# Copying a chunk's two banks of down sums with two engines instead of one

## The chip, the cores and the metric

The kernel runs on one core of a Trainium2 chip. The core has five engines that run side by side, each with its own queue of instructions in program order: TensorE (PE; its weight loads are listed apart as PEld), VectorE (DVE), ScalarE (ACT), GpSimd (POOL) and SyncE (SP). Here SP and POOL issue transfers. The metric is the device time of one execution in microseconds; the time of a kernel is the median over its runs.

## The reference

Two layers in a row, in float32. First an attention through 49 agents for each of 4 batches of 12480 rows of 128 numbers, then a feed-forward layer over all 49920 rows.

```python
def _attn_ref(q, k, v, agents):
    scale = 1.0 / np.sqrt(q.shape[-1])
    ...
    a2k = sm(agents, k)          # softmax over the keys
    agent_v = a2k @ v            # 49 x 128 per batch
    q2a = sm(q, agents)          # softmax over the agents
    return (q2a @ agent_v).astype(np.float32)

def _moe_ref(x, w_in, w_out):
    h = x @ w_in                                  # 128 -> 2048
    g = h * (1.0 / (1.0 + np.exp(-1.702 * h)))
    return (g @ w_out).astype(np.float32)         # 2048 -> 128
```

## The kernel before

The rows are taken in 98 chunks of 512 (`CH`), two chunks to a group. The last chunk has 256 rows. Within a group 16 steps are counted (`NF`), eight to a chunk, and the program is written two steps at a time by `two_steps(t)`. Each step multiplies a chunk's softmaxed queries up to 128 x 2 of the 2048 inner numbers (`up`, PSUM tiles `ph`), ACT applies the gate (`g`, L557), and four steps later (`LAG = 4`) `down` multiplies them back to 128 outputs. The sums of a chunk's eight down steps gather in the PSUM tile `po`.

Products are kept near float32 by splitting an operand in a rounded part and the rest: `gh` is the rounded `g`, made by a POOL transfer (L564) or by an ACT copy (L566), and `gl = g - gh` is made by DVE (L572), 776 times in all. `down` then does three products: `gh` with `wo_h`, `gl` with `wo_h`, `gh` with `wo_l`.

`po` has two banks. PE works with two halves of its rows at once: rows 0 to 63 of the contraction add into bank 0, rows 64 to 127 into bank 1, so a chunk's result is the sum of both banks. `po` has one buffer, so the first `down` of the next chunk can't write before the banks of this one have been read. `store` reads them: ACT copies both (L599, 128 x 1024) into the SBUF tile `o`, SP writes the first half of `o` to memory (L600), and three steps later POOL adds the second half to it in memory with a transfer that accumulates (`store_add`, L605).

The order on each engine is the order in which this Python code runs (`manual_schedule`). Between the last `down` of a chunk and the first of the next, PE has one pair of `up` calls, and at some boundaries more: after an odd chunk the query transposes (L527), after an even chunk the query scores (L216). Other work is put at given steps by `put`: the splits and scores of the queries (L201, L203, L216, L229), the softmax (L503, L507, L513), and for the next batch first the key scores (steps in `K_AT`) and then the value sums (`v_pair`, `e_pair`, `acc`). So an engine's program differs from chunk to chunk, and the same pattern comes three times, once per batch; in the last fifth there is no next batch.

Chunks are counted from 0 below. In DVE's queue the place of `store` lies behind a `gl` of the chunk that ends and ahead of another `gl`, `gl` being made by

```python
    def second(t, f):
        jobs(t + 1)
        if FIRST + 2 <= t < steps + 2:
            do_low(t - 2)
```

which `two_steps` calls between the last two `down` of the chunk; `store` follows both.

Of the kernel before, what the change touches and what calls it, by code (L numbers as in the profile page):

```python
# [45 lines left out]
def kernel(  # L46
# [10 lines left out]
    nc = tc.nc  # L57
# [14 lines left out]
    def width(m):  # L72
        return min(CH, T - m * CH)
# [516 lines left out]
    def store(m, po):  # L590
        n = width(m)
        o = work.tile([P, 2, CH], F32, name="o", tag="o", bufs=1)[:, :, :n]
        out = outT[:, m * CH : m * CH + n]
        if m == NC - 1:
            nc.scalar.copy(out=o[:, 0], in_=po[:, 0, :n])
            nc.vector.tensor_add(out=o[:, 0], in0=po[:, 1, :n], in1=o[:, 0])
            nc.sync.dma_start(out=out, in_=o[:, 0])
            return None
        nc.scalar.copy(out=o, in_=po[:, :, :n])  # L599
        nc.sync.dma_start(out=out, in_=o[:, 0])  # L600
        return o

# [97 lines left out]
    with tc.manual_schedule(engines={E.PE, E.Activation, E.DVE, E.Pool, E.SP}):  # L700
# [9 lines left out]
        for c in range(2):  # L710
            nc.vector.tensor_add(
                out=sel[:, c * H : c * H + A], in0=ident[:, 0:A], in1=ident[:, H : H + A]
# [150 lines left out]
    po = {}  # L863
# [8 lines left out]
    def two_steps(t):  # L872
# [34 lines left out]
        if not downs:  # L907
            second(t, f)
        elif e == NF // 2 - 2:
            put(t + 3, lambda m=m, o=store(m, po.pop(m)): store_add(m, o))  # L910
# [53 lines left out]
```

## Time and profile before

| | us |
|---|---|
| median of 3 runs | 1939.64 |
| lowest and highest run | 1938.58, 1943.8 |
| profiled execution (its span, first to last instruction) | 1941.2 |
| PE busy | 1895.0 (98%) |
| DVE busy | 1538.4 (79%) |
| ACT busy | 1500.1 (77%) |
| POOL busy | 328.2 (17%) |
| chain that ended last: PE's share | 85% |
| mean granted TensorE clock | 0.996 |

The profile is of one execution; its span lies 1.6 us above the median of the runs, and no other time is given for it. Busy time of PE is modelled from its matmuls, which overlap, so 98% doesn't say that PE did all it could. Where PE did nothing while waiting for another engine, the list of waits has it, with the engine and line that ended the wait.

### The profile page before, as it was taken

The page shows a single profiled execution, that of the slowest core. Times are in us where ns is not written, and L with a number is a line of the kernel's source. Part 1 is how long each engine was busy: PE and PEld are TensorE (multiplying, and loading weights), DVE is VectorE, ACT ScalarE, POOL GpSimd, SP SyncE. Part 2 cuts the span into 40 slices and gives each one's busy share as a digit, 9 for nine tenths or more (in the row PEclk, how much of TensorE's full clock was granted, in tenths as well). Part 3 has the DMA queues.
Part 4 walks back from the last instruction along what each step waited for, and adds up shares of the span by engine and source line. Part 5 has one row for each costly group of instructions (what it writes and reads, how often), then busy time and mean ns, then how long its engine had stood idle before and what let it go on. Part 6 is the DMA issues. An engine that isn't in the chain of part 4 may idle for free.

```text
span 1941.2 us, 56369 instructions
## 1 busy us (share of the span) xinstructions
PE 1895.0 (98%) x24100; PEld 1588.5 (82%) x24100; DVE 1538.4 (79%) x1979; ACT 1500.1 (77%) x2414; POOL 328.2 (17%) x583
## 2 busy tenths in 40 slices
PE   7899999999999999999999999999999999999998
PEld 4577788878799998788789999788878888888887
DVE  6798988878688889888778988888877667666665
ACT  3677777887788777877787778777877788888886
POOL 0011111111111111111111111111111111111112
PEclk9999999999999999999999999999999999999999
DMA  8477776776567776776657677777555666666665
GB/s 337 143 220 218 208 195 191 206 202 204 170 205 205 210 209 185 208 205 198 196 175 210 206 211 203 193 202 200 184 169 180 183 193 186 199 188 193 187 181 144
DMA packets 133213, 383.39 MB, mean 198 GB/s; under 512 B 14998, under 2 KB 17174, under 8 KB 132962
## 3 DMA queue, kind: packets, MB, share of 16 engines
q0 software_dynamic: 77264, 253.00, 45.3%
q1 hardware_dynamic: 55697, 126.78, 21.1%
q8 instruction: 189, 3.10, 0.7%
q14 instruction: 63, 0.51, 0.1%
HBM read 81.53 MB, written 50.99 MB: 68 GB/s over the span
## 4 chain that ended last, share of the span: by engine, by line
PE 85%; DVE 5%; ACT 3%; issue 2%; DMA 1%; POOL 0%; ACTq 0%; DVEq 0%; POOLq 0%
PE po L109 52%; PE ph L109 25%; PE ps_m L216 5%; DVE gl L572 2%; PE ps_m L109 1%; ACT g L557 1%; ACT o L599 1%; DMA gh<-g 1%; PE ps_m L473 1%; DVE v_pair L422 1%; DVE rest L203 0%; PE ps_m L527 0%; DVE rest L201 0%; DVE v_pair L421 0%; DVE lo L538 0%
## 5 line engine op out<-in xcount | busy, mean ns | idle before, releaser
L557 ACT ACTIVATE g<-ph 128x512 f32<-128x512 f32 x1568 | 809.4, 605 | 326.4 <-PE ph L109 319.8
L572 DVE TENSOR_TENSOR gl<-g,gh 128x1024 fp32r<-128x1024 f32 x776 | 920.1, 1213 | 58.0 <-DMA gh<-g 38.0
L109 PE MATMUL po<-gh,wo_h 64*128 64x512 f32 (+1 forms) x3104 | 512.8, 400 | 16.6 <-ACT o L599 15.5
L109 PE MATMUL po<-gl,wo_h 64*128 64x512 f32 (+1 forms) x3104 | 502.6, 394 | 1.5 <-DVE gl L572 1.5
L109 PE MATMUL po<-gh,wo_l 64*128 64x512 f32 (+1 forms) x3104 | 498.0, 391 | 0.0
L564 POOL DMA_DIRECT2D gh<-g x436 | 236.5, 542 | 1510.3 <-ACT g L557 1227.5
L566 ACT CAST gh<-g 128x1024 fp32r<-128x1024 f32 (+1 forms) x340 | 359.7, 1058 | 9.2
L109 PEld LDWEIGHTS po<-gl,wo_h 64*128 64x128 f32 x3104 | 311.0, 185 | 58.6 <-DVE gl L572 8.0
L109 PEld LDWEIGHTS po<-gh,wo_l 64*128 64x128 f32 x3104 | 312.8, 185 | 54.2
L109 PEld LDWEIGHTS po<-gh,wo_h 64*128 64x128 f32 x3104 | 296.6, 186 | 68.1 <-ACT o L599 19.1
L109 PE MATMUL ph<-hi,wh 49*128 49x512 f32 (+4 forms) x1616 | 330.3, 388 | 0.0
L109 PE MATMUL ph<-lo,wh 49*128 49x512 f32 (+4 forms) x1616 | 329.6, 388 | 0.0
L109 PE MATMUL ph<-hi,wl 49*128 49x512 f32 (+4 forms) x1616 | 327.5, 384 | 0.0
L109 PEld LDWEIGHTS ph<-hi,wh 49*128 49x128 f32 x1616 | 167.5, 185 | 30.8 <-issue 2.4
L109 PEld LDWEIGHTS ph<-hi,wl 49*128 49x128 f32 x1616 | 166.1, 186 | 26.6 <-issue 0.9
L109 PEld LDWEIGHTS ph<-lo,wh 49*128 49x128 f32 x1616 | 165.7, 184 | 24.9
L599 ACT COPY o<-po 128x1024 f32<-128x1024 f32 x97 | 98.3, 1013 | 53.4 <-PE po L109 53.4
L538 DVE TENSOR_TENSOR lo<-ps_m,hi 128x256 fp32r<-128x256 f32 x98 | 37.0, 420 | 120.7 <-ACT hi L536 120.7
L203 DVE TENSOR_TENSOR rest<-rest 128x512 bf16<-128x512 f32 (+2 forms) x176 | 129.3, 742 | 0.9
L216 PE MATMUL ps_m<-ag_part,rest 64*128 64x49 bf16 x4188 | 118.9, 181 | 5.2 <-DVE rest L203 5.0
L216 PEld LDWEIGHTS <-rest 64*128 64x128 bf16 (+1 forms) x4236 | 109.7, 94 | 6.0 <-DVE rest L203 5.8
L605 POOL DMA_DIRECT2D outT<-o x97 | 84.9, 876 | 93.1 <-DMA outT<-o 80.9
(140 smaller groups left out, 1305.4 us busy)
## 6 DMA issues: line engine op xcount, KB each, us to landing
gh<-g POOLq DMA_DIRECT2D x432, 512.0 KB, 3.5
kt<-kT SPq DMA_DIRECT2D x52, 480.0 KB
outT<-o SPq DMA_DIRECT2D x97, 256.0 KB
outT<-o POOLq DMA_DIRECT2D x97, 256.0 KB, 5.5
qt<-qT SPq DMA_DIRECT2D x94, 256.0 KB
vt<-v SPq DMA_DIRECT2D x39, 480.0 KB
hi<-hi SPq DMA_DIRECT2D x98, 98.0 KB
lo<-lo SPq DMA_DIRECT2D x98, 98.0 KB
```

The lines of the kernel that those rows point to most:

```text
L109: nc.tensor.matmul(out=out, lhsT=lhsT[r], rhs=rhs[r], start=start, stop=stop, tile_position=(k * H, 0))
L203: nc.vector.tensor_sub(out=halves(r)[1][:, s], in0=r[:, s], in1=halves(r)[0][:, s])
L216: nc.tensor.matmul(out=ps[k][o : o + n, j * A : (j + 1) * A], lhsT=x[r, t0 : t0 + n], rhs=ag_part[r, b, y, :], start=(i == 0), stop=(i == ...
L422: nc.vector.tensor_sub(out=vp[:TB, :, C : 2 * C], in0=vt[:TB], in1=vp[:TB, :, 0:C].bitcast(F32))
L473: nc.tensor.matmul(out=pw[:, i * 256 : i * 256 + m], lhsT=w["avT"], rhs=w_in_sb[:, t : t + m], start=True, stop=True)
L538: nc.vector.tensor_sub(out=l, in0=x, in1=h.bitcast(F32))
L557: nc.scalar.activation(out=g[:, k, :n], in_=ph[k][:, :n], func=AF.Gelu_apprx_sigmoid)
L564: nc.gpsimd.dma_start(out=gh, in_=g)
L566: nc.scalar.copy(out=gh, in_=g)
L572: nc.vector.tensor_sub(out=gl, in0=g, in1=gh.bitcast(F32))
L599: nc.scalar.copy(out=o, in_=po[:, :, :n])
L605: nc.gpsimd.dma_start(out=outT[:, m * CH : m * CH + width(m)], in_=o[:, 1], accum_op=ALU.add)
```

## The change

The one copy of both banks by ACT becomes two: ACT copies bank 0, DVE copies bank 1. The transfers out and the last chunk's store are as before. The new line shifts the line numbers behind it by one: the SP store is L601 in the changed kernel, POOL's L606.

```diff
-        nc.scalar.copy(out=o, in_=po[:, :, :n])
+        nc.scalar.copy(out=o[:, 0], in_=po[:, 0, :n])
+        nc.vector.tensor_copy(out=o[:, 1], in_=po[:, 1, :n])
         nc.sync.dma_start(out=out, in_=o[:, 0])
         return o
```

DVE's queue at the end of an odd chunk in the last fifth of the program, before (`p_pad` is the softmax result, `gl` the rest of `g`, `lo` the rest of the transposed queries; names in brackets are the engines and transfer queues whose semaphores an instruction waits for):

```order
L513 TENSOR_TENSOR p_pad<-e_sb,z 128x2x4x49 [waits DVE_49]
L572 TENSOR_TENSOR gl<-g,gh 128x1024 [waits DMASW6_49,PE_49]
L572 TENSOR_TENSOR gl<-g,gh 128x1024 [waits DMASW7_49,PE_49]
L538 TENSOR_TENSOR lo<-ps_m,hi 128x4x64 [waits DMAHW0_49,DMAHW1_49,PE_49,Activation_49]
L538 TENSOR_TENSOR lo<-ps_m,hi 128x4x64
```

And at the same kind of place now:

```order
L513 TENSOR_TENSOR p_pad<-e_sb,z 128x2x4x49 [waits DVE_49]
L572 TENSOR_TENSOR gl<-g,gh 128x1024 [waits DMASW1_49,PE_49]
L600 COPY o<-po 128x512 [waits DMAHW2_49,DMASW7_49,Activation_49]
L572 TENSOR_TENSOR gl<-g,gh 128x1024 [waits DMASW2_49]
L538 TENSOR_TENSOR lo<-ps_m,hi 128x4x64 [waits DMAHW0_49,DMAHW1_49,PE_49,Activation_49]
L538 TENSOR_TENSOR lo<-ps_m,hi 128x4x64
```

The copy stands between two `gl`. It waits for the transfers that read `o` the last time and for ACT; PE isn't among its waits. The count of ACT's semaphore that it waits for is the one that SP's store of bank 0 (L601) waits for, that of ACT's copy.

PE's queue where the next chunk's sums begin, before (`po` is the new chunk's tile; the two rows ahead are the query transposes):

```order
L527 MATMUL ps_m<-ident,p_pad 128x64 [waits DVE_49,PE_49]
L527 MATMUL ps_m<-ident,p_pad 128x64 x7
L109 MATMUL po<-gh,wo_h 128x512 [waits DMASW3_49,Activation_49]
L109 MATMUL po<-gh,wo_h 128x512 x3
L109 MATMUL po<-gl,wo_h 128x512 [waits DVE_49]
L109 MATMUL po<-gl,wo_h 128x512 x3
L109 MATMUL po<-gh,wo_l 128x512 x4
```

And now:

```order
L527 MATMUL ps_m<-ident,p_pad 128x64 [waits DVE_49,PE_49]
L527 MATMUL ps_m<-ident,p_pad 128x64 x7
L109 MATMUL po<-gh,wo_h 128x512 [waits DMASW3_49,DVE_49]
L109 MATMUL po<-gh,wo_h 128x512 x3
L109 MATMUL po<-gl,wo_h 128x512 x4
L109 MATMUL po<-gh,wo_l 128x512 x4
```

The first product of a chunk waited for ACT and waits for DVE now; the products with `gl` have no wait of their own here any more, since DVE's copy stands behind that `gl`. Beside these rows the queues of PE, ACT, DVE, POOL and SP hold the same instructions in the same order, with ACT's copy half as wide.

## Rows read from the trace of the kernel before

**Rows 1.** The page's busy times: us, share of the span, instructions.

```profile
PE 1895.0 (98%) x24100; PEld 1588.5 (82%) x24100; DVE 1538.4 (79%) x1979; ACT 1500.1 (77%) x2414; POOL 328.2 (17%) x583
```

**Rows 2.** PE's waits: who waited for whom, us in total, times, longest us.

```profile
PE po L109 <- ACT o L599: 15.5, 20, 1.7
...
PE po L109 <- DVE gl L572: 1.5, 5, 0.3
```

**Rows 3.** Groups of ACT by line and shape: count, busy us, mean ns, idle before.

```profile
L599 ACT COPY o<-po 128x1024 f32<-128x1024 f32 x97 | 98.3, 1013 | 53.4 <-PE po L109 53.4
...
L292 ACT COPY e_col<-ps_m 120x512 f32<-120x512 f32 x12 | 7.1, 588 | 15.5 <-PE ps_m L290 15.4
```

**Rows 4.** Groups of DVE, the same columns.

```profile
L434 DVE COPY acc<-ps_m 128x514 f32<-128x514 f32 x3 | 2.1, 687 | 0.0
...
L375 DVE COPY run_max<-score 120x392 f32<-120x392 f32 x3 | 1.1, 359 | 0.0
```

**Rows 5.** Timeline, ACT handing to DVE: start, duration, instruction, [idle before <-releaser].

```profile
920.99 0.48 ACT L228 COPY e_sb<-ps_m 128x392 f32<-128x392 f32 x1
...
921.50 0.57 DVE L229 TENSOR_TENSOR e_sb<-ps_m,e_sb 128x392 f32<-128x392 f32 x1 [2.18 <-ACT e_sb L228]
```

**Rows 6.** Timeline at the end of chunk 43, which is odd.

```profile
934.32 2.35 DVE L572 TENSOR_TENSOR gl<-g,gh 128x1024 fp32r<-128x1024 f32 x2
...
936.45 1.01 ACT L599 COPY o<-po 128x1024 f32<-128x1024 f32 x1
...
937.51 0.73 PE L109 MATMUL po<-gh,wo_h 64*128 64x512 f32 x4 [0.74 <-ACT o L599]
```

**Rows 7.** Timeline at the end of chunk 73, odd, in the last fifth.

```profile
1522.01 1.22 DVE L572 TENSOR_TENSOR gl<-g,gh 128x1024 fp32r<-128x1024 f32 x1
...
1523.89 1.01 ACT L599 COPY o<-po 128x1024 f32<-128x1024 f32 x1
...
1524.95 0.73 PE L109 MATMUL po<-gh,wo_h 64*128 64x512 f32 x4
```

**Rows 8.** The same boundary, DVE alone: what follows the two `gl`.

```profile
1527.43 0.76 DVE L538 TENSOR_TENSOR lo<-ps_m,hi 128x256 fp32r<-128x256 f32 x2 [4.21 <-ACT hi L536]
```

**Rows 9.** The last such boundary, chunk 93.

```profile
1878.23 1.00 ACT L599 COPY o<-po 128x1024 f32<-128x1024 f32 x1
...
1879.28 0.49 PE L109 MATMUL po<-gh,wo_h 64*128 64x512 f32 x2
```

**Rows 10.** Timeline at the end of chunk 0.

```profile
88.81 2.35 DVE L572 TENSOR_TENSOR gl<-g,gh 128x1024 fp32r<-128x1024 f32 x2
...
89.01 0.73 PE L109 MATMUL po<-gh,wo_h 64*128 64x512 f32 x4 [1.66 <-ACT o L599]
```

**Rows 11.** Timeline at the end of chunk 3.

```profile
147.96 1.02 ACT L599 COPY o<-po 128x1024 f32<-128x1024 f32 x1 [0.27 <-PE po L109]
...
148.79 2.35 DVE L572 TENSOR_TENSOR gl<-g,gh 128x1024 fp32r<-128x1024 f32 x2
...
149.37 0.48 PE L109 MATMUL po<-gh,wo_h 64*128 64x512 f32 x1
```

**Rows 12.** Timeline at the end of chunk 25.

```profile
584.27 2.35 DVE L572 TENSOR_TENSOR gl<-g,gh 128x1024 fp32r<-128x1024 f32 x2
584.42 1.02 ACT L599 COPY o<-po 128x1024 f32<-128x1024 f32 x1 [0.32 <-PE po L109]
...
585.78 0.48 PE L109 MATMUL po<-gh,wo_h 64*128 64x512 f32 x1
```

**Rows 13.** Timeline at the end of chunk 34, where value sums begin.

```profile
763.14 2.35 DVE L572 TENSOR_TENSOR gl<-g,gh 128x1024 fp32r<-128x1024 f32 x2
...
763.81 0.93 PE L109 MATMUL po<-gh,wo_h 64*128 64x512 f32 x4
```

**Rows 14.** Windows: us, busy us (instructions) per engine, granted clock, DMA share, GB/s.

```profile
760.00:764.00 4.00, 2.47 (x106) 1.92 (x104) 3.96 (x7) 3.54 (x6) 0.53 (x1) 1.00 0.93 294
764.00:768.00 4.00, 4.00 (x22) 3.13 (x22) 3.93 (x6) 0.49 (x1) 0.88 (x1) 0.57 0.83 198
```

## The prediction

> **What bounds the kernel now.** I read the busy times first, then PE's waits, then the timeline at the chunk ends. PE is busy for 1895.0 of 1941.2 us and DVE and ACT for 79% and 77% [rows 1], so PE sets the time and a microsecond counts only where PE has to wait longer or less long. In PE's waits the line that the change touches comes first: 15.5 us over 20 occasions in which the first product of a new chunk waits for ACT's copy L599; DVE's `gl` costs PE next to nothing, 1.5 us [rows 2]. Those 15.5 us are all that a faster emptying of `po` can give back. One of the 20 is the wait of 1.66 us at the start [rows 10], one of 0.4 us lies near the end, and the 18 others are one pattern, 0.74 us each [rows 6]: six odd chunks in each of the three stretches in which the next batch's value sums are made. There ACT comes late, since its copy starts without an idle time before it. 18 times 0.74 is 13.3 us, which with the two others makes the 15.4.
>
> **What the change does to one boundary.** ACT's copy goes from 128 x 1024 to 128 x 512. The old one takes 1.013 us on average; a 512-wide ACT copy out of PSUM is in the trace and takes 0.588 [rows 3]. So the ACT half ends 0.43 us sooner. DVE gets a copy of 512 out of PSUM. The nearest row is a DVE copy of 514 out of PSUM, 0.687 us; the fastest DVE copy rate in the trace is that from SBUF, 392 elements in 0.359, which for 512 would be at most 0.47 [rows 4]. I take 0.69, the row with the same source and size, and keep 0.47 as the low end. The Trainium skill (VectorE: DVE Perf Modes, "Why PSUM operands drop a tier") says that a float32 operand in PSUM holds VectorE to its base rate; the two rows agree with that, and by it alone the low end would fall away.
>
> The two copies look as if they ran side by side. In the new program they don't: DVE's copy waits for ACT's semaphore at ACT's copy, and PE's first product now waits for DVE. The new chain from the start of ACT's copy is therefore 0.59 (ACT), some 0.03 for the handing over (ACT's copy L228 ends at 921.47, DVE's add starts at 921.50 [rows 5]), and 0.69 (DVE): 1.31 us where it was 1.02. The release comes **0.29 us later**, if DVE is free. If DVE is still at work on the `gl` ahead of the copy, it comes later still: 0.69 us after that `gl`, whatever ACT does. PE starts about 0.05 after the release (the old copy ends at 937.46, PE starts at 937.51 [rows 6]).
>
> **The sum over the 97 boundaries**, each by the same rule:
> - The 18 odd chunks with ACT late. The `gl` ahead of the copy is the first of the two at 934.32, done by 935.54, so DVE is waiting when ACT's half ends at 937.04, and its copy ends at 937.76 [rows 6]. PE waits 0.29 more: 18 x 0.29 = 5.2 us.
> - Twelve odd chunks of the last fifth, from 71 to 93. PE starts the new chunk at 1524.95, just 0.05 behind the end of the old copy at 1524.90 [rows 7], and so in the last of them, 1879.28 behind 1879.23 [rows 9]. Nothing is to spare: 12 x 0.29 = 3.5 us.
> - Three odd chunks of the opening, 3, 5 and 7, with DVE late. The first of two `gl` that begin at 148.79 ends near 150.01 (half of the pair); DVE's next instruction starts 0.08 before the end of the last, so the copy runs from 149.93 to 150.62, and PE could start at 150.67 where it started at 149.37: 1.30 each, 3.9 us [rows 11]. Chunk 0 the same way: `gl` until 90.03, PE at 90.69 for 89.01, 1.68 [rows 10]. Chunks 1 and 2 come to 2.0 together.
> - Eight odd chunks like 25 (25 to 31, 49 to 55), where the key scores fill DVE: `gl` until 585.49, PE at 586.15 for 585.78, 0.37 each, 2.9 us [rows 12].
> - Chunks 10, 34, 58 and 40. In 34 the first `gl` ends at 764.36, so PE starts at 765.02 for 763.81, 1.21 [rows 13]; the four together are 3.8 us.
> - The last three and one more: 0.7 us.
> - The other 45 or so, nearly all even: PE has the query scores or the key scores to do between two chunks and reaches the new one later than the new release. They cost nothing.
>
> Together 5.2 + 3.5 + 3.9 + 1.7 + 2.0 + 2.9 + 3.8 + 0.7 = **23.7 us**. With the copy at 0.47 us the same sum is 13.
>
> **What lies beside other work.** ACT gives back 97 x 0.43 = 41 us of busy time, which is worth nothing: it doesn't bring the late copies forward, because between two of them ACT sits idle for PE, 53.4 us ahead of L599 alone [rows 3]. DVE takes on 97 x 0.69 = 67 us, 82% of the span, and also stands still until ACT is done. Behind the waiting copy in its queue is a `gl`, then `lo`, scores or splits. At chunk 73 that `gl` now starts at 1522.01 next to its neighbour and would start near 1525.1, three microseconds later; but the instruction behind it, `lo`, waits for ACT until 1527.43 anyway [rows 7, 8], so the delay ends there. At every boundary I followed the added delay until DVE's next idle time and found no `gl` and no split that PE would have to wait for beyond what the late release already costs. That cover is thinnest at the odd chunks. Queues: the SP store of bank 0 leaves 0.43 us sooner; POOL's accumulating transfer waits for that store's landing and so is not held up by DVE's copy.
>
> The sum stands against the profiled execution of 1941.2 us, and since that lies 1.6 above the median of the runs I add it to the median: 1939.6 + 24 = 1964.
>
> **Rivals.**
> - *The copies overlap after all* (the wait for ACT would be for something older). The Trainium skill (PSUM — Partial Sum Buffer, "Specifications (TRN2)") says that ScalarE and VectorE read PSUM in parallel at full rate if their banks differ, as they do here. No row before shows the two at it; the order of waits speaks against it, not the memory. In numbers of this kernel: at the 18 late chunks the release comes 0.43 sooner, 18 x -0.43 = -7.7; the twelve would not lose their 3.5; the 14.3 us of the chunks where DVE is late stay, since DVE's place in its queue is the same. Net +6.5: 1946.
> - *DVE's lateness spreads, or PE's clock falls.* Where PE had little to do around 762, waiting twice and working on narrow score products, its granted clock went to 1.2 GHz for a while: 0.57 on average from 764 to 768, full before [rows 14]. Such a fall costs (1 - 0.57) x 4 = 1.7 us. The waits of 0.74 didn't bring one, nor did that of 1.66. After the change there are about 25 waits between 1.0 and 3.4 us. If half or all of them brought a fall, that is 20 to 43 us on top; DVE falling behind in the opening, where its slack is smallest, would add some 10. About 1990.
> - *Faster.* The side that could win is the 18 late chunks: ACT's half frees bank 0 at 937.04 instead of 937.46. If the wait for DVE turned out short there (a copy side by side) and the later releases made room in which DVE is no longer behind at the others, -7.7 to at most -15.5 us would be left: 1924 to 1932. It decides as soon as the chunks with DVE late lose less than 7.7 us in all; I count 14.3 for them, and each rests on a `gl` that ends after ACT's half would.
> - *Nothing to measure.* PE's times are modelled and small waits may be absorbed in them; with the overlap above and half of DVE's lateness gone, the sum is near 0: 1940.
>
> **How the numbers follow.** A change of under 0.3%, some 6 us, can't be told from none here. The forecast, 1964, has a chance of 0.62, with 1953 (the quick copy) to 1976 as its own range. DVE or the clock getting worse: 0.17. The overlap: 0.10, half of it within 6 us and half above. Faster: 0.05. Nothing: 0.06. So slower 0.62 + 0.17 + 0.05 = 0.84, the same 0.11, faster 0.05. The range from 1946 to 1988 takes in the overlap and part of the clock case.
>
> **What would show it.** In the changed kernel's profile the DVE copy should take 0.69 us and start right behind the end of ACT's copy at odd chunks; PE's waits for DVE's copy should come to some 40 us (15.5 + 24) in about 50 places, those for ACT's copy should be gone, and the waits for `gl` stay small. If the DVE copies start together with ACT's, the chain is wrong. If PE's waits for `gl` or for the splits grow by more than 5 us, the cover that I counted is not there. If the clock row shows more stretches at half speed than before, the second rival is at work.

## The result and the profile after

| | before | after |
|---|---|---|
| median of 4 runs each, us | 1939.11 | 1967.34 |
| lowest and highest | 1937.99, 1943.8 | 1963.1, 1969.33 |
| ratio, with 95% interval | | 1.0135 [1.0121, 1.0149] |
| profiled execution's span, us | 1941.2 | 1964.9 |

The changed kernel is slower by 28 us at the median. The two profiled spans are only 23.7 us apart, because the profiled execution of before was one of its longer ones. A run's span, from the first to the last instruction, is 1.8 us shorter than its time (1964.9 for the 1966.71 of the profiled run of after), so the 1941.2 us stand for a time of some 1943 us; the difference has to do with PE's clock and is taken up below.

The busy times of after answer to [rows 1]:

```profile
PE 1899.9 (97%) x24100; PEld 1547.2 (79%) x24100; DVE 1601.2 (81%) x2076; ACT 1462.4 (74%) x2414; POOL 326.7 (17%) x583
```

DVE has 97 more instructions and 63 us more of work, ACT 38 us less, and PE's work is the same to 5 us. PE's waits answer to [rows 2] (who waited for whom: us in total, times, longest us):

```profile
PE po L109 <- DVE o L600: 34.2, 41, 3.3
PE ps_m L216 <- DVE rest L203: 3.7, 5, 1.0
...
PE po L109 <- DVE gl L572: 1.1, 4, 0.3
```

The 15.5 us of waiting for ACT's copy are gone from the list, and 34.2 us of waiting for DVE's copy stand in their place, in 41 places instead of 20. Waits for `gl` haven't grown.

The next two fences are ACT's and DVE's copies in the groups by line and shape (columns as in [rows 3]):

```profile
L599 ACT COPY o<-po 128x512 f32<-128x512 f32 x97 | 56.6, 584 | 52.6 <-PE po L109 52.6
```

```profile
L600 DVE COPY o<-po 128x512 f32<-128x512 f32 x97 | 66.7, 688 | 79.9 <-ACT o L599 79.9
```

The last figures of the two lines matter most: how long the engine stood idle ahead of the copies, and what ended it. ACT's copy waits for PE, as before. DVE's copy is put down to ACT alone, 79.9 us over the kernel. So the two copies run one behind the other, and in a timeline this looks as follows. Chunk 43, the boundary of [rows 6]:

```profile
950.02 1.22 DVE L572 TENSOR_TENSOR gl<-g,gh 128x1024 fp32r<-128x1024 f32 x1
...
952.15 0.58 ACT L599 COPY o<-po 128x512 f32<-128x512 f32 x1
...
952.76 0.69 DVE L600 COPY o<-po 128x512 f32<-128x512 f32 x1 [1.52 <-ACT o L599]
...
953.50 0.73 PE L109 MATMUL po<-gh,wo_h 64*128 64x512 f32 x4 [1.03 <-DVE o L600]
```

From the start of ACT's copy to PE's first product it is 953.50 - 952.15 = 1.35 us; in [rows 6] it was 937.51 - 936.45 = 1.06. That is the 0.29 us of the prediction, and PE's wait went from 0.74 to 1.03. DVE had been idle for 1.52 us, waiting for ACT.

To see where the time went, I took the start of the last `down` product of each chunk in either trace and subtracted. The shift grows at few places:

| boundary (chunk that ends) | forecast, us | shift added, us |
|---|---|---|
| ahead of the first chunk boundary | 0 | 1.9 |
| 0, the wait | 1.68 | 1.66 |
| 0, PE at a lower clock behind the wait | 0 | 1.5 |
| 1 and 2 | 2.0 | 1.4 |
| 3, 5, 7 | 3.9 | 3 x 0.65 = 1.95 |
| 18 odd chunks with ACT late, 12 of the last fifth | 8.7 | 8.6 |
| 8 like chunk 25 | 2.9 | 8 x 0.36 = 2.9 |
| 10, 34, 58, 40 | 3.8 | 3.0 |
| 56 and the rest | 0.7 | 1.1 |
| sum | 23.7 | 24.0 |

The sum agrees with the 23.7 us between the spans; 0.2 us come back in the last chunk. The first row lies ahead of any instruction that the change touches, so it is a difference between two executions and not the change. It has to do with PE's clock too. Its granted clock is listed as a share of 2.4 GHz, and at the other level, 1.2 GHz, as 0.5. PE's window from 24 to 28 us (columns as in [rows 14]) was before

```profile
24.00:28.00 4.00, 3.64 (x40) 2.11 (x34) 3.86 (x8) 1.74 (x6) 0.00 (x0) 1.00 1.02 410
```

and after

```profile
24.00:28.00 4.00, 4.00 (x38) 3.76 (x38) 3.79 (x9) 1.88 (x5) 0.00 (x0) 0.57 1.03 411
```

Without the first row and the row on the clock, 20.6 us are left.

The clock of all runs tells the rest. Every timed run lists its mean granted clock. Over 27 timed runs of the kernel before, taken beside the second group of experiments (the 49, chunk 0, ACT twice, DVE everywhere), the mean time is 1939.0 us at 0.999 (6 runs), 1940.2 at 0.998 (8), 1941.1 at 0.997 (6) and 1943.3 at 0.996 (7): about 1.40 us for each 0.001. Their mean clock is 0.9975, their mean time 1940.9. The four runs of after have 0.994, 0.993, 0.996 and 0.992, a mean of 0.9938, and a mean time of 1966.8. The 28 us of the medians are 25.8 between these means, mainly because the median of the four runs of before in the table above lies 1.8 us below the mean of the 27. Of the 25.8 us, 0.0037 x 1400 = 5.2 go with the lower clock, and **20.6 us are left at equal clock**, which is what the table gives too. The 5.2 is an estimate: the runs of before reach from 0.996 to 0.999, and three of the four of after lie below that. I split every run below in the same way.

### The profile page after: what moved, and what is told of

The parts are those of the page before. It is cut to its first block, busy times and chain, and to the rows that moved or that the text cites. A ratio compares the mean times of both kernels' runs of the same rounds, so it can differ in the third digit from the quotient of the medians.

```text
span 1964.9 us, 56509 instructions
## 1 busy us (share of the span) xinstructions
PE 1899.9 (97%) x24100; PEld 1547.2 (79%) x24100; DVE 1601.2 (81%) x2076; ACT 1462.4 (74%) x2414; POOL 326.7 (17%) x583
## 4 chain that ended last, share of the span: by engine, by line
PE 70%; DVE 10%; ACT 9%; issue 5%; DMA 1%; POOL 0%; ACTq 0%; DVEq 0%; POOLq 0%
PE po L109 43%; PE ph L109 20%; PE ps_m L216 5%; ACT g L557 4%; DVE gl L572 4%; PE ps_m L109 2%; DVE o L600 1%; ACT L411 1%; ACT L503 1%; ACT o L599 1%; DMA gh<-g 1%; ACT e_sb L503 1%; ACT score L411 1%; DVE v_pair L422 1%; DVE rest L203 1%
## 5 line engine op out<-in xcount | busy, mean ns | idle before, releaser
L109 PE MATMUL po<-gh,wo_h 64*128 64x512 f32 (+1 forms) x3104 | 505.6, 401 | 36.1 <-DVE o L600 34.2
L109 PEld LDWEIGHTS po<-gh,wo_h 64*128 64x128 f32 x3104 | 284.9, 186 | 97.7 <-DVE o L600 43.2
L109 PEld LDWEIGHTS po<-gl,wo_h 64*128 64x128 f32 x3104 | 297.8, 185 | 67.4 <-DVE gl L572 6.0
L109 PEld LDWEIGHTS po<-gh,wo_l 64*128 64x128 f32 x3104 | 299.5, 185 | 65.1
L109 PE MATMUL ph<-hi,wh 49*128 49x512 f32 (+4 forms) x1616 | 321.3, 388 | 0.3 <-DVE wl L477 0.3
L109 PE MATMUL ph<-lo,wh 49*128 49x512 f32 (+4 forms) x1616 | 320.8, 388 | 0.0
L109 PEld LDWEIGHTS ph<-hi,wh 49*128 49x128 f32 x1616 | 158.6, 184 | 35.8 <-ACT g L557 2.3
L109 PEld LDWEIGHTS ph<-hi,wl 49*128 49x128 f32 x1616 | 157.2, 186 | 31.9 <-issue 0.9
L109 PEld LDWEIGHTS ph<-lo,wh 49*128 49x128 f32 x1616 | 156.8, 184 | 29.9
L600 DVE COPY o<-po 128x512 f32<-128x512 f32 x97 | 66.7, 688 | 79.9 <-ACT o L599 79.9
L203 DVE TENSOR_TENSOR rest<-rest 128x512 bf16<-128x512 f32 (+2 forms) x176 | 129.3, 741 | 0.9
L606 POOL DMA_DIRECT2D outT<-o x97 | 84.9, 875 | 114.6 <-DMA outT<-o 59.0
L599 ACT COPY o<-po 128x512 f32<-128x512 f32 x97 | 56.6, 584 | 52.6 <-PE po L109 52.6
```

The lines of the kernel that those rows point to most:

```text
L109: nc.tensor.matmul(out=out, lhsT=lhsT[r], rhs=rhs[r], start=start, stop=stop, tile_position=(k * H, 0))
L203: nc.vector.tensor_sub(out=halves(r)[1][:, s], in0=r[:, s], in1=halves(r)[0][:, s])
L600: nc.vector.tensor_copy(out=o[:, 1], in_=po[:, 1, :n])
L606: nc.gpsimd.dma_start(out=outT[:, m * CH : m * CH + width(m)], in_=o[:, 1], accum_op=ALU.add)
```

## Experiments

All were timed beside the kernel before, on the same chip; the three groups ran on three chips, and the runs of before in the other two groups lie within 0.3 us of the line through the 27. "At equal clock" is the kernel's mean time less that line, taken at the kernel's own mean clock.

**The sums in two tiles.** `po` becomes two tiles of one bank, so that each copy reads a tile of its own.

```diff
+    def po_banks():
+        return [ps_o.tile([P, 512], F32, name=f"po{k}", tag=f"po{k}") for k in range(2)]
...
-                po[m] = ps_o.tile([P, 2, 512], F32, name="po")
+                po[m] = po_banks()
...
-        nc.scalar.copy(out=o, in_=po[:, :, :n])
+        nc.scalar.copy(out=o[:, 0], in_=po[0][:, :n])
+        nc.vector.tensor_copy(out=o[:, 1], in_=po[1][:, :n])
```

> The sums get two tiles of one bank each instead of one tile of two banks, and the two copies stay with ACT and DVE. In this program each copy waits for PE alone and the first product of a chunk waits for both. Theory (the loss is ACT's copy and DVE's copy in a row, plus DVE being late in its own queue): at the 30 odd boundaries where ACT was the late one the loss of 0.29 us turns into a gain (18 x -0.43, 12 x -0.25), the boundaries with DVE late keep their loss: about +3 to +7 us against the kernel before, 1942 to 1947, and DVE's copies start beside ACT's, not behind them. Rival (DVE's 67 us of added work is what costs, the wait is harmless): still near +28, 1965 or more.

Measured: 1945.39 against 1940.38, ratio 1.0024 [1.0015, 1.0033]; at equal clock -1.4 us, and 5.6 more with a mean clock of 0.9935. The timeline at the end of chunk 43, DVE and ACT:

```profile
938.90 1.22 DVE L577 TENSOR_TENSOR gl<-g,gh 128x1024 fp32r<-128x1024 f32 x1
...
940.04 0.68 DVE L605 COPY o<-po 128x512 f32<-128x512 f32 x1
...
941.03 0.58 ACT L604 COPY o<-po 128x512 f32<-128x512 f32 x1
```

DVE's copy starts right behind its `gl`, 0.99 us ahead of ACT's: it no longer waits for ACT. PE starts at 941.66, 0.05 behind ACT's end. Here the two copies don't meet. At the end of chunk 45 they do:

```profile
981.11 0.69 DVE L605 COPY o<-po 128x512 f32<-128x512 f32 x1 [0.23 <-PE po L114]
...
981.12 0.58 ACT L604 COPY o<-po 128x512 f32<-128x512 f32 x1
```

Side by side they take 0.69 and 0.58 us, as long as when each runs alone. PE's waits in that kernel:

```profile
PE po L114 <- DVE o L605: 6.5, 8, 1.6
...
PE po L114 <- ACT o L604: 5.8, 16, 1.2
```

What follows: DVE waited for ACT because both read the one tile `po`, not because the two can't empty two banks at once. Both copies also write one tile, `o`, and that was left as it was, so it isn't what put them in a row. Without that order the loss at equal clock is gone, but no gain comes out. In the trace the 30 odd chunks with ACT late or nothing to spare win 11.6 us, and the 18 with DVE late lose 11.1, part of it by the clock behind chunk 0.

**The changed copy at some of the boundaries only.** The 30 odd chunks with ACT late or nothing to spare, then all the others:

```diff
+LATE = {*range(9, 20, 2), *range(33, 44, 2), *range(57, 68, 2), *range(71, 94, 2)}
...
-        nc.scalar.copy(out=o, in_=po[:, :, :n])
+        if m in LATE:        # the second kernel: if m not in LATE
+            nc.scalar.copy(out=o[:, 0], in_=po[:, 0, :n])
+            nc.vector.tensor_copy(out=o[:, 1], in_=po[:, 1, :n])
+        else:
+            nc.scalar.copy(out=o, in_=po[:, :, :n])
```

> The two-engine copy of the changed kernel at 30 boundaries only: the odd chunks 9 to 19, 33 to 43, 57 to 67 (ACT late) and 71 to 93 (last fifth); at the other 67 ACT copies both banks as before. Theory: 30 x 0.29 = +8.7 us, 1948, with each DVE copy waiting for ACT, and no more falls of the clock than before. Rival (the wait for ACT costs nothing by itself, all the loss is DVE's lateness elsewhere): within 2 us of the kernel before.

> The complement: the two-engine copy at the other 67 boundaries, ACT alone at those 30. Theory: what is left of the loss, 15 us by the sum of the prediction, 13 to 20 with what the changed kernel showed at chunk 0 (a wait of 3.3 us and a fall of the clock behind it): 1953 to 1959. If the two parts add up, this and the 30 together make the 28 us. Rival (the loss is the 30 boundaries alone): within 3 us of the kernel before.

Measured: the 30 alone give 1947.3 against 1940.38, ratio 1.0033 [1.0021, 1.0046], at equal clock +8.2 us. The other 67 alone give 1958.81, 1.0096 [1.0081, 1.0111], at equal clock +12.6, and 5.9 more with a mean clock of 0.9932. PE's waits with the 30 alone:

```profile
PE po L110 <- DVE o L602: 21.9, 30, 1.1
```

and with the 67 alone:

```profile
PE po L110 <- ACT o L604: 13.3, 18, 0.8
PE po L110 <- DVE o L602: 12.7, 13, 3.3
```

What follows: 8.2 + 12.6 = 20.8 us, and the whole change costs 20.6, so the two sets add up at equal clock and nothing spreads from one to the other. The 30 waits of up to 1.1 us leave the clock as it was (0.9988). The other 67, the wait of 3.3 us among them, lower it.

The 67 can be divided again: without the 18 in which DVE is late, 49 are left, and chunk 0 by itself is one of the 18.

```diff
+DVE_LATE = {0, 1, 2, 3, 5, 7, 10, 25, 27, 29, 31, 34, 40, 49, 51, 53, 55, 58}
...
+        if m not in LATE | DVE_LATE:     # the second kernel: if m == 0
```

> The two-engine copy at the 49 boundaries left over: neither the 30 odd ones of the experiments before nor the 18 at which the sum found DVE late (0, 1, 2, 3, 5, 7, 10, 25, 27, 29, 31, 34, 40, 49, 51, 53, 55, 58); ACT alone at those 48. Theory: PE reaches the next chunk later than the later release, so half of the added DVE work, 34 us, costs under 2 us: 1940 to 1942. Rival (added DVE work spreads through DVE's queue): a share of the loss like the share of the work, 49/97 of 28 us, 1954.

> The two-engine copy at the end of chunk 0 alone. Theory: PE's wait there grows from 1.66 to 3.3 us, and right behind it the granted clock falls to half for a while, at 92 us as in the changed kernel, which costs another 1.6 us: about +3 us, 1943, and a fall at 88 to 95 us in the profile. Rival (the fall has to do with something else): +1.7 us and no fall there.

Measured: the 49 give 1942.69 against 1940.8, ratio 1.0005 [0.9997, 1.0014], at equal clock +0.5: the time lies 0.7 us above the range that was expected, and half of all the boundaries cost next to nothing, as counted. Chunk 0 alone gives 1943.63, 1.0018 [1.0007, 1.0029], at equal clock +1.5, and 2.2 more with a mean clock of 0.9959. PE's longest wait for DVE's copy there is 3.3 us, and the window behind it (columns as in [rows 14]) shows the clock at 0.64:

```profile
88.00:96.00 8.00, 4.68 (x24) 3.50 (x22) 6.45 (x9) 5.12 (x10) 0.53 (x1) 0.64 0.52 156
```

**Two instructions or two engines.** ACT copies both banks, in two instructions:

```diff
-        nc.scalar.copy(out=o, in_=po[:, :, :n])
+        nc.scalar.copy(out=o[:, 0], in_=po[:, 0, :n])
+        nc.scalar.copy(out=o[:, 1], in_=po[:, 1, :n])
```

> ACT copies both banks, in two instructions of 128 x 512, at all boundaries; DVE gets nothing. Theory: the release comes some 0.06 to 0.1 us later than with one instruction (twice 0.587 less the overlap of 0.1), at 30 boundaries that matter: +2 to +3 us, 1942 to 1943; the loss came with the second engine and not with the splitting. Rival (splitting costs): +9 us or more.

Measured: 1944.35 against 1940.8, ratio 1.0012 [1.0000, 1.0024], at equal clock +2.2. The time lies 1.4 us above the range that was expected, the 2.2 within it. In the trace the 30 boundaries lose 0.05 us each, where two copies in a row on two engines lost 0.29.

**DVE copies both banks,** first everywhere:

```diff
-        nc.scalar.copy(out=o, in_=po[:, :, :n])
+        nc.vector.tensor_copy(out=o, in_=po[:, :, :n])
```

> DVE copies both banks in one instruction at all 97 boundaries, ACT none. Theory: the 30 boundaries gain 14 us as when DVE had them alone, and the 18 with DVE late lose more than with half the copy, 14.3 + 18 x 0.53 = 24 us, less the part that the opening gives back (4), and some 2 at even ones where DVE is late too: +8 us, between 1943 and 1956. Rival (a copy on DVE is the faster one everywhere): 1925 or less.

Measured: 1976.0 against 1940.8, ratio 1.0171 [1.0149, 1.0194], at equal clock +22.9 and 11.0 more by the clock. This is a miss by 20 us and more. I had counted with copies that end late where DVE is late; the trace shows late copies in the value stretches too, where DVE should have been free. POOL's waits in that kernel show the way:

```profile
POOL outT L605 <- DMA outT<-o: 123.3, 44, 6.3
...
POOL outT L605 <- DVE gl L572: 72.7, 18, 6.1
...
POOL outT L605 <- DVE lo L538: 32.4, 15, 3.6
```

and one case in POOL's timeline, then in DVE's:

```profile
471.86 0.88 POOL L605 DMA_DIRECT2D outT<-o  x1 [5.40 <-DMA outT<-o]
472.42 0.86 POOL L564 DMA_DIRECT2D gh<-g  x1
```

```profile
479.28 1.23 DVE L572 TENSOR_TENSOR gl<-g,gh 128x1024 fp32r<-128x1024 f32 x1 [4.78 <-PE ph L109]
...
485.62 1.22 DVE L599 COPY o<-po 128x1024 f32<-128x1024 f32 x1
```

A later copy makes SP's store land later. POOL's accumulating transfer of bank 1 waits for that landing, and a `gh` transfer stands behind it in POOL's queue. In all, POOL stands 322 us at L605, where it was 93 before:

```profile
POOL outT L605 <- DMA outT<-o: 80.9, 85, 5.3
```

Of the 322 the list puts 123 down to the landing; what the rows that name DVE waited for can't be told from them. A late `gh` means a late `gl`: the `gl` at 479.28 takes the `gh` issued at 472.42, which landed at 479.16, and its bracket names PE only because PE's semaphore came 0.02 us later. The copy stands behind `gl`: at the end of chunk 19 it starts 3.69 us behind the end of the sums. If that is the cause, putting POOL's transfer two steps later must take it away. The changed kernel got the same edit, as a control:

```diff
-            put(t + 3,
+            put(min(t + 5, steps + LAG + 1),
```

> DVE copies both banks at all 97 boundaries, as in the run that came out at 1976, and POOL's accumulating transfer stands two steps later in its queue (five behind the chunk's end, not three). In that run POOL waited 123 us for the stores' landings and some 200 us more at that transfer, with the transfers that make gh queued behind it. Theory (those late gh are what made gl late in the value stretches, and with it DVE): POOL's waits at the accumulating transfer fall to less than half, DVE's copy no longer starts 2 to 4 us behind the end of odd chunks there, and the time falls by 10 us or more, to 1955 to 1965. Rival (DVE is late by its own work): within 4 us of that run, 1972 or more.

> The changed kernel with the accumulating transfer two steps later in POOL's queue. Theory (its loss is made at the boundaries by ACT's and DVE's copies in a row and by DVE's place, not in POOL's queue): within 3 us of the changed kernel, 1964 to 1970. Rival (POOL's queue has a part in it, as where DVE copied both): 1960 or less.

Measured: 1958.39 against 1942.74 with DVE copying both, ratio 1.0085 [1.0070, 1.0100] for 1.0171 without the edit. The same boundary now reads

```profile
480.18 1.21 DVE L599 COPY o<-po 128x1024 f32<-128x1024 f32 x1
```

0.38 us behind the end of the sums, and POOL waits about 8 us at the transfer in all. At equal clock +7.3 us are left of the 22.9, close to the 8 that I had counted; 9.8 more go with a mean clock of 0.9905. The changed kernel stays at 1966.3 against 1942.74, 1.0136 [1.0115, 1.0157], at equal clock +20.8 where it was 20.6. So POOL's queue made 15.6 us of the miss, most of the rest goes with the clock by the line, and the queue has no part in what the change itself costs.

**DVE copies both banks at the 30 alone,** the version that the readings point to: there DVE is idle and ACT is late.

```diff
+        copy = nc.vector.tensor_copy if m in LATE else nc.scalar.copy
+        copy(out=o, in_=po[:, :, :n])
```

> At the same 30 boundaries DVE copies both banks in one instruction of 128 x 1024 and ACT none; ACT as before at the other 67. Theory: at these boundaries DVE stands idle before ACT gets to its copy, so DVE's 1.22 us can begin at the end of the chunk (or behind a gl, 0.4 to 0.9 us later) and ends 0.3 to 0.7 us ahead of ACT's old copy: 15 x -0.7, 3 x -0.3 and 12 x -0.25 make about -14 us, 1925. If instead DVE's added 1.2 us makes gl late for PE, it is no faster than before and PE's waits for gl grow from 1.5 us to 10 or more.

Measured: 1925.34 against 1940.38, ratio 0.9922 [0.9908, 0.9935], at equal clock -15.3. It beats both kernels. PE's waits and the end of chunk 43:

```profile
PE po L110 <- ACT o L601: 2.0, 2, 1.7
...
PE po L110 <- DVE o L601: 1.3, 3, 0.4
...
PE po L110 <- DVE gl L573: 1.1, 4, 0.3
```

```profile
929.39 1.22 DVE L573 TENSOR_TENSOR gl<-g,gh 128x1024 fp32r<-128x1024 f32 x1
930.53 1.22 DVE L601 COPY o<-po 128x1024 f32<-128x1024 f32 x1
...
931.80 0.73 PE L110 MATMUL po<-gh,wo_h 64*128 64x512 f32 x4
```

DVE's copy of both banks takes 1.22 us, longer than ACT's 1.01, and still PE starts without a wait, since the copy starts right behind `gl` and not when ACT gets to it. The waits for `po` fell by 12.6 us (15.5 + 1.5 to 2.0 + 1.3 + 1.1). The rest of the 15.3 comes from where the list of waits has nothing. At the 12 odd chunks of the last fifth PE starts 0.25 us sooner each, 2.9 us in all; before, the modelled records of PE's query transposes reached up to that start, so no idle time showed (the last row of [rows 7] has no brackets). The 18 others win 12.6 us in the trace.

## Why the prediction was right, and where it wasn't

**The order of the two copies: right.** It rested on the waits in the instruction order, and both the timeline and DVE's 79.9 us of waiting for ACT show it. The rival in which the copies overlap falls for the kernel as it is; with two tiles it holds, and then the time at equal clock is nearly that of before.

**The release 0.29 us later, on 30 boundaries: right.** 8.7 forecast, 8.6 in the trace, 8.2 measured by themselves. The price of DVE's copy (0.69) came from a row of the same source and nearly the same size; it is 0.688. PE's waits for the copy came to 34.2 us in 41 places, not to some 40 in about 50: the eight chunks like 25 grow by 0.36 us each, but the list has no wait there.

**"All that a faster emptying can give back": too small.** The prediction took the 15.5 us of listed waits for the whole of it. DVE's copy at the 30 boundaries won 2.9 us where no wait was listed.

**The cover on DVE: right.** Most of the added work and waits, 94 us of them, came out of DVE's idle time ahead of `lo`. Before, in the groups of DVE:

```profile
L538 DVE TENSOR_TENSOR lo<-ps_m,hi 128x256 fp32r<-128x256 f32 x98 | 37.0, 420 | 120.7 <-ACT hi L536 120.7
```

and after:

```profile
L538 DVE TENSOR_TENSOR lo<-ps_m,hi 128x256 fp32r<-128x256 f32 x98 | 37.0, 420 | 26.7 <-ACT hi L536 26.6
```

One sentence of that part is wrong: it has POOL's accumulating transfer not held up by DVE's copy, and at four places it was. A row of POOL's waits in after:

```profile
POOL outT L606 <- DVE o L600: 8.0, 4, 3.1
```

It cost PE nothing that the runs show, since with that transfer two steps later the time stayed.

**The boundaries with DVE late: right in kind, too large in size.** Forecast 15.0 us with the last row of the sum, 12.0 in the trace, 12.1 as 12.6 less the 0.5 of the 49. The largest error is chunks 3, 5 and 7: 1.30 forecast, 0.65 measured. The release is 1.29 us later there, as worked out, but PE didn't lose all of it. In the trace before, the first product with `gl` of the new chunk and the `up` that comes next in PE's timeline were

```profile
150.06 0.73 PE L109 MATMUL po<-gl,wo_h 64*128 64x512 f32 x4
...
152.49 0.40 PE L109 MATMUL ph<-hi,wh 49*128 49x512 f32 x2
```

and after

```profile
157.22 0.73 PE L109 MATMUL po<-gh,wo_h 64*128 64x512 f32 x4 [1.04 <-DVE o L600]
157.79 0.63 PE L109 MATMUL po<-gl,wo_h 64*128 64x512 f32 x4
...
160.12 0.40 PE L109 MATMUL ph<-hi,wh 49*128 49x512 f32 x2
```

From PE's first product to that `up` it was 152.49 - 149.37 = 3.12 [rows 11] and is 160.12 - 157.22 = 2.90. Before, PE got through early and was then held up by `gl`; since DVE's copy stands behind that `gl`, `gl` is done when PE starts now. The wait was in part moved, not added. Further on in these chunks PE's waits for DVE's splits (L203) got shorter too, 0.2 us for 0.5 a pair. The step that failed is "PE could start at 150.67 where it started at 149.37: 1.30 each": it took the later start for the loss, without following PE to the end of the chunk. Chunks 1, 34, 58 and 40 were sized by the same rule, and came out at 0.5, 1.2, 0.4 and 0; there the difference was not followed.

**The clock: left to a rival, and partly true.** The second rival had a chance of 0.17 and spoke of 20 us and more, if half or all of some 25 waits brought a fall of the clock. There are 25 waits of 1.0 us or more, and in the profile one has a fall behind it that the kernel before didn't have at the same place, at chunk 0. What came is about 5.2 us. Its sentence that a wait of 1.66 us brought no fall is true of the profile before, but not of every execution: with DVE copying at the 30 boundaries, PE's wait there is 1.65 us and the window reads

```profile
88.00:96.00 8.00, 6.35 (x40) 4.83 (x38) 4.16 (x6) 7.21 (x13) 0.55 (x2) 0.79 0.52 174
```

PE's window from 88 to 96 us before:

```profile
88.00:96.00 8.00, 6.99 (x60) 5.67 (x62) 6.33 (x9) 7.77 (x14) 0.53 (x1) 1.00 0.46 151
```

and after:

```profile
88.00:96.00 8.00, 4.68 (x28) 3.60 (x26) 5.48 (x8) 6.09 (x11) 0.53 (x1) 0.79 0.61 187
```

In the timeline of after, the product with four matmuls that follows the wait takes 1.22 us, where it takes 0.73 elsewhere:

```profile
92.61 1.22 PE L109 MATMUL po<-gh,wo_h 64*128 64x512 f32 x4 [3.32 <-DVE o L600]
93.62 1.06 PE L109 MATMUL po<-gl,wo_h 64*128 64x512 f32 x4
...
96.59 0.63 PE L109 MATMUL po<-gh,wo_l 64*128 64x512 f32 x4
```

So the forecast of 1964 came within 3.3 us of 1967.34 with two errors against each other: 3 us too much for DVE's lateness, and 5 us of clock that weren't in the sum. That it came so close is in part luck; the mechanism is not.

## What to carry to other kernels

Two engines that read one PSUM tile can be put one behind the other by the program, so look at what the second copy waits for before counting with half the time; two tiles took the wait away here. Who should empty a tile is a question of the single boundary: the engine that stands idle there, not the one with the shorter copy, and the same edit was worth -15 us at 30 boundaries and +16 when made at all of them with its side effect on a queue removed (as timed; at equal clock -15.3 and +7.3). A list of waits can miss one: 2.9 of those 15 us came from places where it showed none. A later start of PE is a loss only as far as the end of the chunk shows it; follow it past the next wait.

## What the runs showed of the hardware

PE's clock differs from one execution to the next of the same kernel: 0.996 to 0.999 before, worth 1943.3 to 1939.0 us. The waits of a kernel go with that: of the profiles in which PE waits 3.3 us or more at the end of chunk 0, all six have the window from 88 to 96 us below full clock (0.64 to 0.79); of the five with a wait of 1.65 to 1.72 one has (0.79), and the kernel with two tiles, with waits of 1.22 and 1.60 us in a row there, has it too (0.79). Whether a certain wait brings a fall in a given execution stays open. Thirty waits of up to 1.1 us, spread over the kernel, brought none that the mean shows (0.9988).

ACT and DVE can read two banks of PSUM at the same time without slowing each other: 0.58 and 0.69 us side by side at chunk 45, in the kernel with two tiles.
